# Fused attention and feed-forward kernel: last store by whole rows behind one copy, first scores of both heads of a pair in one step, another order of the first batch's steps

## The chip, the cores and the metric

The kernel runs on one core of one Trainium2 chip. The metric is the device time of one execution in microseconds; the median of three runs before the change is 719.26 us (718.98 to 720.36).

A core has five engines with a queue of instructions each, worked off in order: TensorE (PE, matrix products; its weight loads are listed as PEld), VectorE (DVE), ScalarE (ACT), GpSimd (POOL) and SyncE (SP), which issues all DMA transfers here. Transfers are carried by 16 DMA engines. The engines wait for each other on semaphores. SBUF is the memory on the core with 128 partitions; PSUM holds the results of matrix products, in eight banks.

## The reference

```
p_packed = sm_attn(p, k, v)                 # 32 packed rows per head attend to 576 keys
out      = sm_attn(q, p_packed, p_packed)   # 576 queries attend to the 32 packed rows
x  = out as (8 * 576 tokens, 8 heads * 64)
h  = x @ w_in                               # 512 -> 2048
g  = h * sigmoid(1.702 * h)
return g @ w_out                            # 2048 -> 512
```

`sm_attn` is softmax attention with scale 1/8; there are 8 batches, 8 heads of width 64 and sequence 576. Everything is float32 in DRAM.

## The kernel before

Work goes batch by batch, b = 0 to 7. For each batch the first attention gives the packed rows P (scores1, an exponential, transposes into aT, `pack`, `pack_end`, a transpose into PT), the second gives the attention weights (scores2, maxima, subtraction, exponential, sums, division, transpose). The attention's output isn't formed: PT times w_in is computed instead (`m_chunk`, four chunks fc of 512 columns), and the hidden layer h (128 hidden columns f by 288 tokens, a half) is the product of that with the transposed attention weights (`h_mm`, L561). The gate is a tanh on ScalarE and one VectorE operation. `out_mm` (L621) multiplies the gated values of one f with the rows f of w_out and adds into one of four PSUM banks of 128 tokens each, over f = 0 to 15.

A value that enters the large products is split into an upper part and the rest (`*_upper`, `*_lower`, names ending in hi and lo), and each product is done as three.

576 tokens are four blocks of 128 and 64 more. The 64 left over of two batches make a fifth block (`h_over`, `over_mm`, pairs 0 to 3); its product lands in one bank, `over_take` copies it to SBUF in two halves of 256 columns, and `over_store` stores each half for both batches.

The weights arrive as 64-bit integers' worth of raw bits: `load_w` issues a transfer, `begin_w` (ScalarE) converts the upper bits into a tile `top`, `join_w` (VectorE) puts the value together. Weights are numbered in the order of their queue: 0 to 3 are chunk 0 of w_in, 4 to 7 rows 0 to 3 of w_out, 8 to 11 chunk 1, 12 to 15 rows 4 to 7, 16 to 19 chunk 2, and so on. Weights 0 to 3 come in two halves of columns.

All order is written by hand: `order` is a list of some 2800 steps (a function and its arguments), and a step puts its instructions on the queues of the engines. A step's last argument, such as `dve`, names the engine that does it; otherwise the function's own default holds (ScalarE for copies, POOL for the lower parts). `warm` steps are products without use, on TensorE only; they stand in the first batch. SyncE's queue is in the order of the `load` and `store` steps too, and a transfer into a buffer that is still read waits there with all behind it.

The names used below: `scores1_first` (L247 through `mm1`) computes the first batch's scores of one head of each pair and one half of the keys; `max1_first` L272, `bias1` L302, `exp1_first` L311 turn them into exponentials; `turn1_mm` L337 and `turn1_copy` make aT; `pack` L370; `pack_end` L383 normalises; `scores2_mm` L451, `scores2_turn` L462, `max2` L482, `sub2` L486, `exp2` L490, `sum2` L495, `norm2` L501, `turn2` L507. Copies show as L116 (ScalarE) or L118 (VectorE), conversions of weights as L205, joins as L217.

Of the kernel before, what the change touches and what calls it, by code (L numbers as in the profile page):

```python
# [21 lines left out]
def kernel(  # L22
# [628 lines left out]

    def over_take(pair, k, engine=nc.scalar):
        if k == 0 or pair == B // 2 - 1:
            taken["over"] = o_tile(f"o_over_{pair}_{k}")
        taken["over", pair, k] = o = taken["over"][:, columns(k)]
        move(engine, o, accs[0][:, columns(k)])

    def over_store(pair, k):
        rest = out.rearrange("(b s) d -> b s d", s=S)[2 * pair : 2 * pair + 2, S - REST :, columns(k)]
        nc.sync.dma_start(rest, taken["over", pair, k])  # L660
# [8 lines left out]
        (warm, 2, 3), (warm, 4, 2), (load, "k", 0, 0), (load, "k", 0, 1), (scores1_first, 0, 0),  # L669
        (max1_first, 0, 0), (warm, 6, 2), (scores1_first, 0, 1), (scores1_first, 1, 0),  # L670
        (max1_first, 0, 1), (load_w, 1, 0), (bias1, 0, 0), (exp1_first, 0, 0),
        (scores1_first, 1, 1), (max1_first, 1, 1), (exp1_first, 0, 1), (max1_first, 1, 0),
        (bias1, 0, 1), (sum1, 0, 0), (turn1_mm, 0, 0), (turn1_copy, 0, 0, dve), (load, "v", 0, 0),
        (exp1_first, 1, 0), (exp1_first, 1, 1), (sum1, 0, 1), (load, "v", 0, 1), (warm, 10, 3),
        (turn1_mm, 0, 1), (turn1_last_mm, 0), (turn1_last_copy, 0), (turn1_copy, 0, 1, dve),
        (load_w, 0, 0), (pack, 0, 0, late), (pack, 0, 1), (begin_w, 0, 0), (join_w, 0, 0),
        (pack_end, 0), (pack_turn_mm, 0), (load_w, 2, 0), (begin_w, 2, 0), (join_w, 2, 0),
        (load, "q", 0, 0), (pack_turn_copy, 0), (scores2_mm, 0, 0), (begin_w, 1, 0),
        (load, "q", 0, 1), (join_w, 1, 0), (warm, 7, 3), (scores2_turn, 0, 0, 0),
        (scores2_turn, 0, 0, 1), (max2, 0, 0, 0), (max2, 0, 0, 1), (load_w, 3, 0), (load_w, 3, 1),  # L680
        (begin_w, 3, 0), (sub2, 0, 0, 0, pool), (exp2, 0, 0, 0), (begin_w, 3, 1),
        (scores2_mm, 0, 1, late), (scores2_turn, 0, 1, 0), (join_w, 3, 0),
        (m_chunk, 0, 0, early, 0), (m_upper, 0, 0, 1, 0), (warm, 3, 3), (sub2, 0, 0, 1, pool),
        (scores2_turn, 0, 1, 1), (sum2, 0, 0, 0), (warm, 5, 2), (max2, 0, 1), (join_w, 3, 1),
        (norm2, 0, 0, 0, pool), (turn2, 0, 0, 0), (load_w, 0, 1), (begin_w, 0, 1), (load_w, 4),
        (exp2, 0, 0, 1), (sum2, 0, 0, 1), (warm, 8, 3), (load_w, 6), (begin_w, 4), (join_w, 4),
        (load_w, 1, 1), (sub2, 0, 1, None, pool), (norm2, 0, 0, 1, pool), (a_upper, 0, 0, 0),
        (a_lower_mm, 0, 0, 0, bank_b), (exp2, 0, 1), (sum2, 0, 1), (load_w, 2, 1),
        (turn2, 0, 0, 1), (upper_w, 4), (begin_w, 1, 1), (a_lower_copy, 0, 0, 0),
        (m_upper, 0, 0, 0, 0), (warm, 0, 3), (warm, 9, 3), (m_lower, 0, 0, 0, 0),  # L690
        (a_upper, 0, 0, 1), (a_lower_mm, 0, 0, 1, bank_b), (a_lower_copy, 0, 0, 1),
        (m_lower, 0, 0, 1, 0), (h_mm, 0, 0, 0), (join_w, 0, 1), (norm2, 0, 1, None, pool),
        (turn2, 0, 1), (lower_w, 4), (begin_w, 2, 1), (join_w, 2, 1), (h_tanh, 0, 0, 0),
        (a_upper, 0, 1, None), (a_lower, 0, 1), (h_mm, 0, 1, 0), (h_tanh, 0, 1, 0), (load_w, 5),
        (begin_w, 5), (join_w, 1, 1), (h_gate, 0, 0, 0), (h_gate, 0, 1, 0), (load, "k", 1, 0),
        (h_upper, 0, 0, 0), (h_lower, 0, 0, 0), (m_chunk, 0, 0, (bank_b, bank_b), 1), (load_w, 11),
        (m_upper, 0, 0, 0, 1), (join_w, 5), (upper_w, 5, dve), (m_lower, 0, 0, 0, 1),
        (h_upper, 0, 1, 0), (m_upper, 0, 0, 1, 1), (load_w, 9), (h_mm, 0, 0, 1), (h_tanh, 0, 0, 1),
# [688 lines left out]
```

## Time and profile before

| | |
|---|---|
| runs | 718.98, 719.26, 720.36 us |
| profiled execution: device time / span | 720.15 / 718.4 us |
| granted TensorE clock, mean | 0.995 |
| VectorE, ScalarE, POOL busy | 56%, 39%, 20% of the span |
| read from DRAM, written | 45.60 MB, 9.44 MB |

```profile
DVE  3978885436554366335635457643775547755541
DMA  9787503310203103121110400213210100010001
## 3 DMA queue, kind: packets, MB, share of 16 engines
q1 hardware_dynamic: 17232, 55.05, 22.0%
## 6 DMA issues: line engine op xcount, KB each, us to landing
v<-v SPq DMA_DIRECT2D x8, 1024.0 KB, 5.3
o<-o SPq DMA_DIRECT2D x32, 256.0 KB, 2.3
k<-pk SPq DMA_DIRECT2D x8, 640.0 KB, 3.9
k<-pk SPq DMA_DIRECT2D x8, 576.0 KB, 5.2
```

The first two lines are the busy share in tenths over 40 slices of 18 us each. VectorE and the DMA engines are busiest in the first slices, where weights and the first batch's inputs arrive. The last part lists transfers: what goes where, how many, the size of one, and the median time from issue to landing.

A row of a timeline reads: start, length (us), engine, line, operation, output<-input, shapes, number of instructions merged, and in brackets the idle time before it with what ended it. A float32 product is two instructions, so a `warm` step of 3 shows as x6.

### The profile page before, as it was taken

The numbers are of one execution on the slowest core, as the hardware profiler recorded it, in microseconds if no ns is written. First come the engines' busy times: TensorE is split into PE (matmuls) and PEld (weight loads), VectorE is DVE, ScalarE is ACT, GpSimd is POOL, SyncE is SP. The second block draws the span as 40 slices with busy tenths as digits, with TensorE's granted clock in tenths as the row PEclk, the third lists the DMA queues.
The fourth block names the chain that finished last, engine by engine and source line by source line (L and its number), as shares of the span: only waits on it lengthen the run. The fifth ranks groups of instructions, "written<-read, shape, count | busy, mean of one in ns | idle before, by whom it ended". The sixth has DMA issues, their size and how long they took to land.

```text
span 718.4 us, 13002 instructions
## 1 busy us (share of the span) xinstructions
PE 701.6 (98%) x5092; PEld 569.6 (79%) x5092; DVE 404.4 (56%) x1026; ACT 278.2 (39%) x672; POOL 145.7 (20%) x171
## 2 busy tenths in 40 slices
PE   7999999999999999999999999999999999999994
PEld 5767778878888888888787788877888878888883
DVE  3978885436554366335635457643775547755541
ACT  3777645423323334453322433433342433333220
POOL 1733433122501223222332123102100000000000
PEclk9999999999999999999999999999999999999998
DMA  9787503310203103121110400213210100010001
GB/s 319 311 307 253 189 0 129 96 38 1 81 17 120 39 8 131 43 88 49 60 52 3 165 0 1 96 34 119 69 49 23 66 18 1 16 44 1 1 16 58
DMA packets 17292, 55.87 MB, mean 78 GB/s; under 512 B 1872, under 2 KB 3920, under 8 KB 16208
## 3 DMA queue, kind: packets, MB, share of 16 engines
q1 hardware_dynamic: 17232, 55.05, 22.0%
q8 instruction: 40, 0.66, 0.4%
q14 instruction: 20, 0.16, 0.1%
HBM read 45.60 MB, written 9.44 MB: 77 GB/s over the span
## 4 chain that ended last, share of the span: by engine, by line
PE 93%; DVE 2%; DMA 2%; ACT 1%; issue 0%; SPq 0%; ACTq 0%
PE acc L621 48%; PE h L561 28%; PE acc_over L621 6%; PE psm_None L399 4%; PE pspv L370 2%; DMA raw<-w_in 2%; PE ps L247 1%; PE ps L451 1%; PE pst L337 1%; DMA k<-pk 1%; PE warm L124 1%; ACT top L205 0%; DVE wo L229 0%; DVE w_in L217 0%; DVE mx L482 0%
## 5 line engine op out<-in xcount | busy, mean ns | idle before, releaser
L621 PE MATMUL acc<-wo,ghi 128*128 128x512 f32 x1024 | 323.9, 397 | 1.5 <-DVE ghi L118 0.8
L621 PEld LDWEIGHTS acc<-wo,ghi 128*128 128x128 f32 x1024 | 179.3, 188 | 42.6 <-issue 14.5
L621 PE MATMUL acc<-wo,glo 128*128 128x512 f32 x512 | 201.9, 394 | 0.1
L569 ACT ACTIVATE g<-h 128x288 f32<-128x288 f32 x256 | 104.0, 411 | 242.3 <-PE h L561 226.9
L551 DVE SCALAR_TENSOR_TENSOR g<-g,h 128x288 f32<-128x288 f32 (+1 forms) x256 | 105.4, 416 | 159.0 <-ACT g L569 158.2
L548 POOL TENSOR_TENSOR glo<-g,ghi 128x224 fp32r<-128x224 f32 (+1 forms) x122 | 93.3, 775 | 307.9 <-ACT ghi L116 201.7
L561 PE MATMUL h<-ahi,mhi 128*128 128x288 f32 x512 | 145.5, 299 | 0.9 <-DVE g L551 0.6
L561 PE MATMUL h<-ahi,mlo 128*128 128x288 f32 x512 | 143.0, 295 | 0.0
L621 PEld LDWEIGHTS acc<-wo,glo 128*128 128x128 f32 x512 | 96.1, 188 | 24.0 <-DVE glo L548 0.9
L561 PEld LDWEIGHTS h<-ahi,mhi 128*128 128x128 f32 x512 | 96.2, 188 | 17.9 <-DVE x L462 5.4
L561 PE MATMUL h<-alo,mhi 128*128 128x288 f32 x512 | 108.6, 293 | 0.0
L561 PEld LDWEIGHTS h<-ahi,mlo 128*128 128x128 f32 x512 | 96.3, 188 | 7.0
L116 ACT CAST ghi<-g 128x224 fp32r<-128x224 f32 (+1 forms) x159 | 62.5, 405 | 59.5 <-DVE g L551 37.1
L561 PEld LDWEIGHTS h<-alo,mhi 128*128 128x128 f32 x512 | 82.0, 188 | 0.2 <-POOL alo L530 0.2
L548 DVE TENSOR_TENSOR glo<-g,ghi 128x224 fp32r<-128x224 f32 (+1 forms) x134 | 59.0, 450 | 17.5 <-ACT ghi L116 14.6
L551 DVE SCALAR_TENSOR_TENSOR over<-g,h 128x64 f32<-128x64 f32 x128 | 27.4, 215 | 35.1 <-ACT g L569 34.8
L427 DVE TENSOR_TENSOR mlo<-psm_None,mhi 128x512 fp32r<-128x512 f32 x62 | 42.0, 683 | 5.3 <-ACT mhi L116 4.8
L621 PE MATMUL acc_over<-wo,ghi_over 128*128 128x512 f32 x128 | 39.8, 392 | 0.0
L116 ACT CAST mhi<-psm_None 128x512 fp32r<-128x512 f32 x45 | 26.1, 586 | 30.3 <-PE psm_None L399 30.3
L118 DVE CAST ghi<-g 128x224 fp32r<-128x224 f32 (+1 forms) x97 | 31.6, 333 | 5.6 <-PE acc L621 2.4
L399 PE MATMUL psm_None<-w_in,PT 64*32 64x512 f32 x496 | 34.0, 596 | 0.0
L621 PEld LDWEIGHTS acc_over<-wo,ghi_over 128*128 128x128 f32 x128 | 23.6, 188 | 4.7
(85 smaller groups left out, 498.3 us busy)
## 6 DMA issues: line engine op xcount, KB each, us to landing
q<-q SPq DMA_DIRECT2D x16, 576.0 KB, 5.8
v<-v SPq DMA_DIRECT2D x8, 1024.0 KB, 5.3
o<-o SPq DMA_DIRECT2D x32, 256.0 KB, 2.3
raw<-w_out SPq DMA_DIRECT2D x16, 511.8 KB, 8.2
raw<-w_in SPq DMA_DIRECT2D x12, 511.8 KB, 7.5
k<-pk SPq DMA_DIRECT2D x8, 640.0 KB, 3.9
k<-pk SPq DMA_DIRECT2D x8, 576.0 KB, 5.2
raw<-w_in SPq DMA_DIRECT2D x8, 255.8 KB, 9.8
```

The source lines that it names most:

```text
L116: nc.scalar.copy(dst, src)
L118: engine.tensor_copy(dst, src)
L124: nc.tensor.matmul(t[:, :P], ident, ident, start=True, stop=True)
L247: nc.tensor.matmul(bank[32 * j : 32 * j + 32, :NH], kq["p", b][rows(eo), j, :], kq["k", b][rows(eo), half, j, :], start=True, stop=True,)
L370: nc.tensor.matmul(bank[32 * j : 32 * j + 32, e * D : (e + 1) * D], aT[:kk, c, e, 32 * j : 32 * j + 32], vt[:kk, c, e0 : e0 + D], start=(c ...
L399: nc.tensor.matmul(banks[eo][32 * j : 32 * j + 32, columns(part)], PT[rows(eo), j, :], w_in_sb[fc][rows(eo), j, columns(part)], start=True ...
L427: nc.vector.tensor_tensor(lo, bank[:, at], hi.bitcast(F32), op=ALU.subtract)
L548: engine.tensor_tensor(lo, src, hi.bitcast(F32), op=ALU.subtract)
L551: nc.vector.scalar_tensor_tensor(dst, th, 1.0, h, op0=ALU.add, op1=ALU.mult)
L561: nc.tensor.matmul(h[:, :NH], m[eo][part][:, fo : fo + P], a[:, eo * NH : (eo + 1) * NH], start=(n == 0), stop=(n == len(terms) - 1),)
L569: nc.scalar.activation(g, st["h", b, f, half][:, :NH], AF.Tanh, scale=1.702)
L621: nc.tensor.matmul(acc, gp[:, at : at + P], wo[f][:, part, :], start=(start and i == 0), stop=(stop and i == 2),)
```

## The change

Three things change.

`over_take` makes one copy of the whole bank, 128 partitions by 512 columns, on VectorE. `over_store` stores for one batch 64 whole rows, from 64 partitions. Before it stored 256 columns of both batches' 64 rows.

`scores1_first` takes only the half of the keys and alternates between the two heads of each pair, as `scores1_mm` of the later batches does.

The list of steps up to about step 320 of 2806 is in another order, and 22 of its copies, casts and subtractions go to another engine. It holds the same steps otherwise, with the same number of `warm` products, all of them ahead of the first `h_mm` as before. Behind that the list is the same but for `over_take`.

```
-    def scores1_first(eo, half):
+    def scores1_first(half):
...
-        for j in range(NP):
-            mm1(0, eo, half, bank, j)
-        st["bank", eo, half] = bank
+        for eo in range(2):
+            if half == 0:
+                new1(0, eo)
+            st["bank", eo, half] = (bank_acc(half) if eo else bank_b)(f"ps1_0_{eo}_{half}")
+        for j in range(NP):
+            for eo in range(2):
+                mm1(0, eo, half, st["bank", eo, half], j)
...
-    def over_take(pair, k, engine=nc.scalar):
-        if k == 0 or pair == B // 2 - 1:
-            taken["over"] = o_tile(f"o_over_{pair}_{k}")
-        taken["over", pair, k] = o = taken["over"][:, columns(k)]
-        move(engine, o, accs[0][:, columns(k)])
+    def over_take(pair, engine=nc.scalar):
+        taken["over"] = o_tile(f"o_over_{pair}")
+        move(engine, taken["over"], accs[0])

     def over_store(pair, k):
-        rest = out.rearrange("(b s) d -> b s d", s=S)[2 * pair : 2 * pair + 2, S - REST :, columns(k)]
-        nc.sync.dma_start(rest, taken["over", pair, k])
+        at = (2 * pair + k + 1) * S - REST
+        nc.sync.dma_start(out[at : at + REST, :], taken["over"][k * REST : (k + 1) * REST, :])
...
-        (warm, 2, 3), (warm, 4, 2), (load, "k", 0, 0), (load, "k", 0, 1), (scores1_first, 0, 0),
+        (warm, 8, 3), (warm, 2, 3), (load, "k", 0, 0), (load, "k", 0, 1), (scores1_first, 0),
+        (max1_first, 0, 0), (load, "v", 0, 0), (load, "v", 0, 1), (scores1_first, 1),
...
+        (h_over, 0, 3), (m_upper, 0, 1, 1, None), (load_w, 17),
...
-        (store, 7, 1), (over_take, 3, 0), (over_take, 3, 1, dve), (over_store, 3, 1),
-        (over_store, 3, 0),
+        (store, 7, 1), (over_take, 3, dve), (over_store, 3, 1), (over_store, 3, 0),
```

SyncE's queue at the end of the program, before: the last two ordinary stores, then the two of the fifth block.

```order
L641 DMA o<-o_2_7711 128x512
L641 DMA o<-o_3_7731 128x512
L641 DMA o<-o_0_7703 128x512
L641 DMA o<-o_1_7705 128x512
L660 DMA o<-o_over_1_7778 2x64x256
L660 DMA o<-o_over_0_7776 2x64x256
```

And changed:

```order
L639 DMA o<-o_2_7708 128x512
L639 DMA o<-o_3_7728 128x512
L639 DMA o<-o_0_7700 128x512
L639 DMA o<-o_1_7702 128x512
L655 DMA o<-o_over_7773 64x512 x2
```

The place and the number of stores are the same; their shape is 64x512 instead of 2x64x256, and both read one tile.

VectorE in the first batch, before, from the weight joins (w_in<-raw) ahead of the first scores2 transpose to the transpose of the first normalised quarter (xt). The names: ps are scores2 in PSUM, x their transpose, mx, sm, rs the maxima, sums and reciprocals; 0_0 and 0_1 are the two halves of the queries.

```order
L217 SCALAR_TENSOR_TENSOR w_in_79<-raw_127,top_84 128x256
L462 STREAM_TRANSPOSE x_0_0_237<-ps_0_0_0_238 128x288
L462 STREAM_TRANSPOSE x_0_0_237<-ps_0_0_1_239 128x288
L482 TENSOR_REDUCE mx_0_0_257<-x_0_0_237 128x9 x2
L462 STREAM_TRANSPOSE x_0_1_267<-ps_0_1_0_268 128x288
L217 SCALAR_TENSOR_TENSOR w_in_79<-raw_260,top_86 128x256
L462 STREAM_TRANSPOSE x_0_1_267<-ps_0_1_1_269 128x288
L495 TENSOR_REDUCE sm_0_0_299<-x_0_0_237 128x9
```

And changed, the same stretch, from the two joins ahead of the first transpose:

```order
L217 SCALAR_TENSOR_TENSOR w_in_79<-raw_231,top_83 128x256
L217 SCALAR_TENSOR_TENSOR w_in_79<-raw_160,top_84 128x256
L460 STREAM_TRANSPOSE x_0_0_244<-ps_0_0_0_245 128x288
L480 TENSOR_REDUCE mx_0_0_256<-x_0_0_244 128x9
L460 STREAM_TRANSPOSE x_0_0_244<-ps_0_0_1_246 128x288
L480 TENSOR_REDUCE mx_0_0_256<-x_0_0_244 128x9
L217 SCALAR_TENSOR_TENSOR w_in_79<-raw_240,top_83 128x256
L217 SCALAR_TENSOR_TENSOR w_in_79<-raw_240,top_86 128x256
L493 TENSOR_REDUCE sm_0_0_282<-x_0_0_244 128x9
L494 TENSOR_SCALAR sm_0_0_282<-sm_0_0_282 128x9
L495 RECIPROCAL rs_0_0_283<-sm_0_0_282 128x9
L460 STREAM_TRANSPOSE x_0_1_288<-ps_0_1_0_289 128x288
```

The transposes of the second half (x_0_1) moved behind the two joins of the fourth weight block (raw_240) and the first sums. On TensorE scores2 of the second half (ps_0_1) stands behind the first `m_chunk` now, where it stood ahead of it. A little further on, `m_upper` of one head, a cast of 128x256, has come to VectorE ahead of the first xt.

TensorE from the last hidden product of f = 5 (h_1_5) to the second batch's second scores (ps_1_0_1), before; acc are the banks of the output, ghi and glo the two parts of the gated values of the f named behind, wo the weights.

```order
L561 MATMUL h_1_5_702<-alo_1_386,mhi_1_1_574 128x288
L621 MATMUL acc_0_460<-wo_627,ghi_4_654 128x512 x2
L621 MATMUL acc_0_460<-wo_627,glo_4_655 128x512
L621 MATMUL acc_0_496<-wo_627,ghi_4_654 128x512 x2
L621 MATMUL acc_0_496<-wo_627,glo_4_655 128x512
L247 MATMUL ps_1_0_1_739<-k_404 32x288
```

And changed, from the same hidden product on, without the repeats of the scores:

```order
L559 MATMUL h_1_5_693<-alo_1_388,mhi_1_1_601 128x288
L619 MATMUL acc_0_437<-wo_560,ghi_3_610 128x512 x2
L619 MATMUL acc_0_437<-wo_560,glo_3_611 128x512
L619 MATMUL acc_0_502<-wo_560,ghi_3_610 128x512 x2
L619 MATMUL acc_0_502<-wo_560,glo_3_611 128x512
L247 MATMUL ps_1_0_1_712<-k_535 32x288
```

Ahead of these scores the changed list has no product of f = 4 left; before, the two shown and one ahead of the hidden product stood there. The first now comes right behind the scores.

More of the change, by code (lines that the diff above doesn't have):

```diff
@@ L675 @@
[L675 to L698, printed above, removed]
@@ new lines @@
+        (pack, 0, 1), (pack_end, 0), (pack_turn_mm, 0), (load_w, 0, 0), (pack_turn_copy, 0, dve),
+        (begin_w, 1, 0), (load, "q", 0, 0), (begin_w, 0, 0), (join_w, 0, 0), (load_w, 3, 0),
+        (load_w, 3, 1), (join_w, 1, 0), (scores2_mm, 0, 0), (scores2_turn, 0, 0, 0),
+        (max2, 0, 0, 0), (scores2_turn, 0, 0, 1), (max2, 0, 0, 1), (warm, 4, 2), (begin_w, 3, 1),
+        (join_w, 3, 1), (warm, 6, 2), (begin_w, 3, 0), (join_w, 3, 0), (m_chunk, 0, 0, early, 0),
+        (sub2, 0, 0, 0, pool), (exp2, 0, 0, 0), (sum2, 0, 0, 0), (load, "q", 0, 1),
@@ new lines @@
+        (load_w, 11), (begin_w, 11), (join_w, 11), (load_w, 10), (begin_w, 10), (join_w, 10),
+        (load, "k", 1, 0), (scores1_mm, 1, 0, inner), (h_upper, 0, 2, 0), (scores1_max, 1, 0, 0),
+        (lower_w, 6), (h_upper, 0, 2, 1), (h_lower, 0, 2, 1), (scores1_copy, 1, 0, 0),
+        (scores1_max, 1, 0, 1), (upper_w, 7), (lower_w, 7), (scores1_copy, 1, 0, 1),
+        (m_chunk, 0, 1), (m_upper, 0, 1, 0, None, dve), (m_lower, 0, 1, 0), (h_mm, 0, 3, 0),
+        (h_tanh, 0, 3, 0), (h_gate, 0, 3, 0), (h_mm, 0, 3, 1), (out_mm, 0, 2, 3),
@@ new lines @@
+        (h_gate, 2, 4, 1), (h_mm, 2, 5, 0), (h_tanh, 2, 5, 0), (h_gate, 2, 5, 0),
+        (h_lower, 2, 4, 0), (h_mm, 2, 5, 1), (h_tanh, 2, 5, 1), (h_gate, 2, 5, 1), (h_over, 2, 5),
+        (h_upper, 2, 5, 0, dve), (over_store, 0, 1), (h_upper, 2, 5, 1, dve),
+        (h_lower, 2, 5, 1, dve), (out_mm, 2, 4, 0), (h_upper, 2, 4, 1), (h_lower, 2, 5, 0, dve),
+        (m_chunk, 2, 2), (load, "k", 3, 1), (scores1_mm, 3, 1, inner), (scores1_max, 3, 1, 1),
+        (m_upper, 2, 2, 0, None), (m_lower, 2, 2, 0), (bias1, 3, 1), (scores1_copy, 3, 1, 0),
@@ new lines @@
+        (m_chunk, 6, 1), (m_upper, 6, 1, 0, None, dve), (scores1_max, 7, 0, 1),
+        (m_upper, 6, 1, 1, None, dve), (m_lower, 6, 1, 1), (store, 5, 0), (m_lower, 6, 1, 0),
+        (out_mm, 6, 1, 1), (out_mm, 6, 2, 1), (h_mm, 6, 3, 1), (out_mm, 6, 1, 2),
+        (scores1_copy, 7, 0, 1), (out_mm, 6, 2, 2), (h_tanh, 6, 3, 1), (h_gate, 6, 3, 1),
+        (h_over, 6, 3), (out_mm, 6, 1, 3), (out_mm, 6, 2, 3), (h_mm, 6, 4, 0), (h_mm, 6, 3, 0),
+        (h_tanh, 6, 4, 0), (h_gate, 6, 4, 0), (h_tanh, 6, 3, 0), (h_gate, 6, 3, 0),
```

250 lines of the change are left out of this document (121 added, 129 removed).

## The prediction

> **What bounds the kernel now.** I read the page first, then busy time by stretch, then the end of the chain of waits, then the engines' timelines of the first 60 us.
>
> ```profile
> span 718.4 us, 13002 instructions
> PE 701.6 (98%) x5092; PEld 569.6 (79%) x5092; DVE 404.4 (56%) x1026; ACT 278.2 (39%) x672; POOL 145.7 (20%) x171
> ```
>
> ```profile
> 0.00:30.00 30.00, 25.29 (x263) 1.00 0.95 354
> 30.00:60.00 30.00, 28.51 (x192) 1.00 0.79 273
> 300.00:500.00 200.00, 199.79 (x1508) 1.00 0.18 60
> ```
>
> TensorE is the bound, and in the middle it is full: 199.79 us busy of 200. Nothing done there for other engines can move the end. What can be won lies in three places: before TensorE starts the long run of products (4.7 us not busy in the first 30), in its pauses between 30 and 60 us (1.5 us), and the time behind its last product (from 708.8 to 718.4, next rows). The profiled run took 720.15 us, 0.9 above the median of 719.26; I work out differences on the profiled run and apply their sum to the median.
>
> **The tail: one copy, two stores of whole rows.** First the end of the chain of waits, then the timeline of the copy and of SyncE's issues:
>
> ```profile
> 697.74 11.02 PE acc_over L621 x48
> 708.82 0.38 ACT o_over L116
> 709.23 0.42 DVE o_over L118
> ```
>
> ```profile
> 700.51 0.68 DVE L118 COPY o<-acc 128x512 f32<-128x512 f32 x1
> 701.22 1.31 SPq L641 DMA_DIRECT2D o<-o  x3
> 709.68 1.14 SPq L660 DMA_DIRECT2D o<-o_over  x2
> ```
>
> The last product ends at 708.8. The two half-width copies run one behind the other (the VectorE copy starts when the ScalarE copy ends) and are done at 709.65, 0.83 us after the first began. One full-width VectorE copy has a row: 0.68. So the issue can begin at 709.5, 0.15 earlier. What follows is larger. The transfers in quarter-microsecond stretches (us, clock, share of the 16 DMA engines, GB/s):
>
> ```profile
> 710.65:710.90 0.25, 1.00 0.06 16
> 716.65:716.90 0.25, 0.50 0.14 49
> 717.15:717.40 0.25, 0.50 0.00 0
> ...
> 702.00:702.25 0.25, 1.00 0.81 303
> 703.75:704.00 0.25, 1.00 1.04 393
> ```
>
> The last stores start moving about 1.0 us after SyncE began the first issue and then crawl for 6.3 us at a share of 0.13 to 0.14, which is two engines' worth of sixteen, and 49 GB/s. Three ordinary stores (128 rows of 2 KB, issued at 701.22) move at 393 GB/s. The last two have the shape 2x64x256, the ordinary ones 128x512. The new ones are 64x512. No store of that shape is in the trace, but a load is, with nothing queued behind it:
>
> ```profile
> 366.47 0.52 SPq L152 DMA_DIRECT2D v<-v_last  x1
> ...
> 368.50:368.75 0.25, 1.00 0.14 49
> 368.75:369.00 0.25, 1.00 0.00 0
> ```
>
> That load is 128 KB, 64 partitions by 512. At 49 GB/s it would need 2.7 us; it is over 2.3 us after its issue began, of which about 0.9 passes before data move. So a 64x512 transfer isn't held to two engines. I take 393 GB/s for the new stores: 0.33 us each. First issue at 709.5, second at 710.0 (0.52 each, by the row of the load), its data from 711.0 to 711.35. From the last byte (716.95) to the end of the span pass 1.45 us, which stay. End at 712.8 instead of 718.4: **-5.6 us**. Ends of the range: 393 GB/s and shorter issues give -6.0; the old rate with only the copy's gain gives -0.15.
>
> [...]
>
> The same two edits for pairs 0 to 2 cost nothing: one 0.68 copy takes the place of a 0.42 and a 0.37, in stretches where TensorE is full. If that cover were gone each would be worth about 0.1 us.
>
> **The head, up to the first hidden-layer product (L561, at 26.60 now).** TensorE's work is the same set of products in both, so after that point only pauses can differ.
>
> ```profile
> 4.77 1.18 PE L247 MATMUL ps<-k 64*32 64x288 f32 x8 [0.91 <-DMA k<-pk]
> 7.04 2.17 PE L247 MATMUL ps<-k 64*32 64x288 f32 x24
> 13.40 2.53 PE L370 MATMUL pspv<-v,aT 128*32 128x64 f32 x80
> 37.97 0.71 PE L247 MATMUL ps<-k 64*32 64x288 f32 x16
> ```
>
> ```profile
> 9.10 0.50 ACT L311 ACTIVATE x<-ps,nb 128x288 f32<-128x288 f32 x1 [6.67 <-DVE nb L302]
> 16.00 0.31 ACT L383 ACTIVATE pn<-pspv,rs 128x64 f32<-128x64 f32 x1 [0.76 <-PE pspv L370]
> 16.90 1.11 ACT L205 CAST top<-raw 128x256 f16<-128x256 bf16 x2
> ```
>
> ```profile
> 4.50:5.00 0.50, 1.00 1.11 433
> ```
>
> Scores: 32 instructions take 1.18 + 2.17 = 3.35 us with one head at a time; 16 with both heads alternating take 0.71 in the second batch. But the early clock is slower, by the means of the same 128x128 product in two windows:
>
> ```profile
> L124 PE MATMUL warm<-ident 128*128 128x128 f32 x6 | 1.5, 421 | 0.0
> L124 PE MATMUL warm<-ident 128*128 128x128 f32 x12 | 1.5, 275 | 0.0
> ```
>
> So 0.71 becomes about 1.1 there (x 421/275). The first half of the keys lands at 4.77 as now. The second half (576 KB behind it, at 433 GB/s) lands near 6.1, while TensorE uses it only at 7.04 now. So the second half's scores start 0.9 us earlier, take 0.35 longer than one head's, and the first exponential moves from 9.10 to about 8.5. From there to the second half of the packed product the steps are the same, on other queues: three warm products still lie between the two sets of transposes, and the aT copies go to ScalarE, which is free there. I take -0.5 us for the end of that product: normalising its second half (16.00) begins at 15.5. Ends: -1.5 (keys at 5.9, the clock faster sooner) to +0.3 (keys just before 7.04).
>
> Of the loads only the order changes: v goes ahead of the weight halves. The queue is full either way (share 0.95, 354 GB/s in the first 30 us, above): the 3.8 MB up to q's first half take 10.8 us, the next 1.1 MB (two weight halves, q's second half) 3.1 more, so both are there before their products at about 16.6 and 20.6. That costs nothing; were the queue 4 us later, the second would.
>
> Then VectorE decides, which had no pause from 17.42 on:
>
> ```profile
> 17.42 0.42 DVE L217 SCALAR_TENSOR_TENSOR w_in<-raw,top 128x256 uint32<-128x256 uint32 x1 [0.28 <-ACT top L205]
> 17.86 0.85 DVE L462 STREAM_TRANSPOSE x<-ps 128x288 f32<-128x288 f32 x2
> 19.37 0.48 DVE L462 STREAM_TRANSPOSE x<-ps 128x288 f32<-128x288 f32 x1
> 25.40 0.42 DVE L507 STREAM_TRANSPOSE xt<-x 128x288 f32<-128x288 f32 x1
> 44.07 0.33 DVE L118 CAST ghi<-g 128x288 fp32r<-128x288 f32 x1
> ...
> 18.57 0.71 PE L451 MATMUL ps<-q,PT 64*32 64x288 f32 x16
> 20.22 0.62 PE L399 MATMUL psm<-w_in,PT 64*32 64x256 f32 x4 [0.52 <-DVE w_in L217]
> 26.60 0.30 PE L561 MATMUL h<-ahi,mhi 128*128 128x288 f32 x1
> ```
>
> Two weight conversions, 1.11 on ScalarE, now come behind the second normalising activation, and their joins, 0.42 each on VectorE, ahead of the first score transpose: 15.5 + 0.3 + 1.1 + 0.84 = 17.75, against 17.86 now. The 0.5 won before is spent. From that transpose to the last one before the hidden layer VectorE now needs 25.40 - 17.86 = 7.54 us. It gets one cast more (m_upper of a half chunk, 128x256, priced at the 0.33 of a 128x288 cast). It also gets a wait. The second scores2 product now stands behind the first m_chunk, whose last pair needs the join of the fourth weight block, at about 20.1 by VectorE's queue; its 0.6, then 0.8 from the scores' start to their transpose (18.57 to 19.37) give 21.4, when VectorE has been free for 0.5 us. Queued behind that transpose are the maximum, the cast, the transpose of the normalised quarter and both sums; POOL's next subtraction waits with them. Sum: -0.1 + 0.33 + 0.5 = +0.7 us, first hidden product at 27.3. Ends: -0.8 (no wait, lead kept) to +1.5.
>
> **The pauses after it.**
>
> ```profile
> 50.74 0.50 PE L621 MATMUL acc<-wo,ghi 128*128 128x512 f32 x1 [0.71 <-POOL wo L229]
> 53.74 0.73 PE L621 MATMUL acc<-wo,ghi 128*128 128x512 f32 x2 [0.78 <-DVE ghi L118]
> 51.37 2.03 ACT L205 CAST top<-raw 128x512 f16<-128x512 bf16 x3 [2.41 <-DMA raw<-w_in]
> ```
>
> The pauses, 0.71 and 0.78, are the whole 1.5 us that TensorE misses between 30 and 60. Both belong to products of f = 4, whose weights or hidden values stood on POOL and VectorE behind joins and casts, and these behind ScalarE conversions that waited for weight loads (2.41 us in the third row). In the changed order the f = 4 products come only after the second batch's second scores, and two weight loads of the third chunk (17 and 18) are issued ahead of those that wait for a buffer (12 to 15). I take both pauses as gone: **-1.5 us**. Ends: -2.2 (0.6 more from the scores there, whose 16 instructions are stretched) to +1.0, if the new order waits for something else.
>
> **Sum.** -5.6 + 0.7 - 1.5 = -6.4 us. On the median: 719.26 - 6.4 = **712.9 us**.
>
> **Rivals.**
> 1. *The head gives nothing or loses.* VectorE's queue ahead of the hidden layer loses the 1.5 us and the pauses come back elsewhere: +1.5 and -0.5, so -4.6 and 714.7; with a new 1 us pause 716. For it speaks that VectorE has no idle row there; against it that it sheds two aT copies (0.68 each, by the copy of that shape above).
> 2. *The head gains more.* The lead of the scores is kept (-0.8) and the pauses go (-2.2): 710.7. Needs scores that are done well before 7.0.
> 3. *The stores stay on two engines.* Then only the copy is won, -0.15, with the head's -0.8: 718.3. Their 2 KB rows could halve the 6.3 us: 715. The 64x512 load speaks against it.
> 4. *Slower.* TensorE's early products are slow (421 against 275 ns) and its stream there is thinner now: alternating scores finish sooner, so it idles longer. If it stays slow into the dense part from 27 us, every us of old work costs 0.5 more. It eats the -6.4 and shows as slower only when some 15 us of that part's work run slow, which gives about 721. The granted clock reads 1.00 in both windows, so only such means show it. Against it: the 275 ns are from 23.8 to 25.5 us, when TensorE still runs mostly filler; the 421 ns are from 2.1 to 2.9. A small chance. [...]
>
> **How the numbers follow.** Forecast 66%, at 712.9 with its own range 711.2 to 714.3. Rival 1 14%, rival 2 13%, rival 3 5% (half of it at 718.3, half near 715), rival 4 2%. The range 710.6 to 715.6 takes in rival 2 and most of rival 1 and leaves out 2 in 10, as sizes in the head are worked out over many short steps. A measurement tells about 0.2% (1.4 us) from no change; below 717.8 is faster: 94%. Within 0.2%: 4%, from rival 3 and a mix of 3 and 1. Slower: 2%.
>
> **What would show it.** Right: a share near 1.0 of the DMA engines for under 1 us after the last copy, the span ending about 3 us after that copy; first L561 near 27.3; no L229 or ghi pause of TensorE between 45 and 55 us. Wrong: a share of 0.13 again after the last product; L561 before 26 or after 28.5; new pauses over 0.5 us between 30 and 75 us; 128x128 products at 421 ns past 20 us.

## The result and the profile after

| | before | after |
|---|---|---|
| median of four runs each, us | 719.51 (718.98 to 720.36) | 715.05 (714.48 to 715.8) |
| profiled execution: device time / span | 720.15 / 718.4 | 715.8 / 714.0 |

The ratio is 0.9938, with an interval of 0.992 to 0.9955: 4.5 us faster, where 6.4 were forecast.

The page of the changed kernel, its first lines, and TensorE's busy time by stretch (from:to in us, length, busy us, number of instructions, clock, share of the DMA engines, GB/s):

```profile
span 714.0 us, 12980 instructions
...
PE 700.0 (98%) x5092; PEld 568.5 (80%) x5092; DVE 404.5 (57%) x1027; ACT 276.1 (39%) x668; POOL 144.7 (20%) x170
```

```profile
0.00:30.00 30.00, 23.79 (x271) 1.00 0.96 366
30.00:60.00 30.00, 29.86 (x209) 1.00 0.75 266
60.00:100.00 40.00, 38.05 (x324) 1.00 0.41 146
300.00:500.00 200.00, 199.25 (x1499) 1.00 0.18 60
```

TensorE is still the bound. Between 30 and 60 us it now misses 0.14 us instead of 1.5. But between 300 and 500 it misses 0.75 instead of 0.21: something was lost in the part that was taken as full.

**The tail.** VectorE's copy and SyncE's issue in the timeline, then the last stretches with DMA traffic (busy times of the five engines, clock, DMA share, GB/s):

```profile
708.86 0.40 PE L619 MATMUL acc_over<-wo,glo_over 128*128 128x512 f32 x1
709.34 0.69 DVE L118 COPY o_over<-acc_over 128x512 f32<-128x512 f32 x1 [6.57 <-PE acc_over L619]
710.06 1.11 SPq L655 DMA_DIRECT2D o<-o_over  x2
```

```profile
711.25:711.50 0.25, 0.00 (x0) 0.00 (x0) 0.00 (x0) 0.00 (x0) 0.00 (x0) 1.00 0.90 205
...
712.00:712.25 0.25, 0.00 (x0) 0.00 (x0) 0.00 (x0) 0.00 (x0) 0.00 (x0) 1.00 1.06 221
712.25:712.50 0.25, 0.00 (x0) 0.00 (x0) 0.00 (x0) 0.00 (x0) 0.00 (x0) 1.00 0.71 156
```

All 16 engines work (share 0.9 to 1.06 instead of 0.13), as forecast, but at 205 to 221 GB/s, about half of the 393 that the forecast took. The last product ends at 709.25 and the span at 714.02: 4.8 us, where 9.6 stood before and 4.0 were forecast.

**The head.** TensorE's first products (the row at 25.25 is the first hidden product), then VectorE's transposes from the first scores2 to the last one ahead of the hidden layer:

```profile
4.86 1.21 PE L247 MATMUL ps<-k 64*32 64x288 f32 x16 [0.57 <-DMA k<-pk]
6.25 1.21 PE L247 MATMUL ps<-k 64*32 64x288 f32 x16 [0.18 <-DMA k<-pk]
...
11.46 1.73 PE L368 MATMUL pspv<-v,aT 128*32 128x64 f32 x80
25.25 0.29 PE L559 MATMUL h<-ahi,mhi 128*128 128x288 f32 x1
```

```profile
8.37 0.50 ACT L309 ACTIVATE x<-ps,nb 128x288 f32<-128x288 f32 x1 [5.94 <-DVE nb L300]
13.45 0.52 ACT L381 ACTIVATE pn<-pspv,rs 128x64 f32<-128x64 f32 x2 [1.51 <-DVE rs L326]
...
15.54 0.48 DVE L460 STREAM_TRANSPOSE x<-ps 128x288 f32<-128x288 f32 x1
24.05 0.42 DVE L505 STREAM_TRANSPOSE xt<-x 128x288 f32<-128x288 f32 x1
```

The first exponential is at 8.37 (forecast 8.5). The two normalising activations stand in one row, from 13.45 to 13.97; the second, for which 15.5 was forecast, starts near 13.66 (16.00 before). The 80 products of `pack` take 1.73 us instead of 2.53, because products of the same shape turn faster from about 10 us on instead of 15: TensorE's clock rose earlier, as "The early clock" below reads it. VectorE's stretch from 15.54 to 24.05 is 8.51 us long (forecast 7.54 + 0.33 + 0.5 = 8.37). So the first hidden product comes 1.35 us earlier than before, not 0.7 later.

**The pauses.** Those at 50.74 and 53.74 are gone. Two others stand in the second batch's first attention, where the kernel before had none (in e1_again, the same kernel once more, only the second is left, with 0.46 us):

```profile
67.67 0.66 PE L335 MATMUL pst<-ident,x 128*128 128x128 f32 x4 [0.47 <-ACT x L316]
72.09 1.15 PE L368 MATMUL pspv<-v,aT 64*32 64x64 f32 x48 [0.79 <-ACT aT L116]
```

**Where the lead goes.** Each batch has one packed transpose (`pspt`). Its start is a mark in the stream of TensorE, and the start of the last pair's `acc_over` products is the last mark. One such row of the changed kernel:

```profile
74.07 0.27 PE L387 MATMUL pspt<-ident,pn 128*128 128x128 f32 x1
```

| start, us | batch 2 | batch 3 | batch 5 | batch 7 | batch 8 | last acc_over |
|---|---|---|---|---|---|---|
| before | 76.29 | 157.76 | 324.42 | 492.65 | 588.49 | 697.57 |
| after | 74.07 | 155.78 | 322.87 | 492.56 | 588.76 | 698.03 |
| after less before | -2.22 | -1.98 | -1.55 | -0.09 | +0.27 | +0.46 |

A lead of 2.2 us at 74 us is a lag of 0.5 at 697. Part of it goes in one step at 376 us, part in an even creep. In sum the span is 4.4 us shorter: 4.9 from the tail, less 0.5. The early lead differs between executions of one kernel, the loss behind it hardly: e1_again leads by 3.13 at the second batch (73.16) and by 0.52 at the end (697.05), a loss of 2.6 where this execution loses 2.7.

The step has these rows, VectorE's and TensorE's, in the changed kernel:

```profile
376.23 0.67 PE L247 MATMUL ps<-k 64*32 64x288 f32 x2
376.34 0.69 DVE L118 COPY o_over<-acc_over 128x512 f32<-128x512 f32 x1 [2.59 <-PE acc_over L619]
376.94 0.44 DVE L549 SCALAR_TENSOR_TENSOR g<-g,h 128x288 f32<-128x288 f32 x1
...
377.44 0.47 PE L247 MATMUL ps<-k 64*32 64x288 f32 x7 [0.55 <-DVE g L549]
```

Pair 1's copy of the fifth block waits on VectorE for the last `acc_over` product, and a gate (g) is queued behind it. The second head's scores need the PSUM bank that this gate reads. Before, the copy's first half ran on ScalarE and its second half stood behind the gate, so the gate was free of it.

### The profile page after: what moved, and what is told of

The parts are those of the page before. It is cut to its first block, busy times and chain, and to the rows that moved or that the text cites. A ratio compares the mean times of both kernels' runs of the same rounds, so it can differ in the third digit from the quotient of the medians.

```text
span 714.0 us, 12980 instructions
## 1 busy us (share of the span) xinstructions
PE 700.0 (98%) x5092; PEld 568.5 (80%) x5092; DVE 404.5 (57%) x1027; ACT 276.1 (39%) x668; POOL 144.7 (20%) x170
## 4 chain that ended last, share of the span: by engine, by line
PE 91%; DVE 4%; DMA 2%; ACT 1%; issue 0%; SPq 0%; DVEq 0%; ACTq 0%
PE acc L619 48%; PE h L559 28%; PE acc_over L619 6%; PE psm_None L397 4%; PE pspv L368 2%; DMA raw<-w_out 1%; PE ps L247 1%; PE ps L449 1%; PE pst L335 1%; DVE w_in L217 1%; DMA k<-pk 1%; ACT top L205 1%; DVE x L460 0%; DVE wo L229 0%; PE warm L124 0%
## 5 line engine op out<-in xcount | busy, mean ns | idle before, releaser
L546 POOL TENSOR_TENSOR glo<-g,ghi 128x288 fp32r<-128x288 f32 (+1 forms) x119 | 89.7, 764 | 313.4 <-ACT ghi L116 205.5
L116 ACT CAST ghi<-g 128x288 fp32r<-128x288 f32 (+1 forms) x161 | 63.3, 406 | 60.5 <-DVE g L549 37.9
L546 DVE TENSOR_TENSOR glo<-g,ghi 128x288 fp32r<-128x288 f32 (+1 forms) x137 | 60.4, 451 | 18.8 <-ACT ghi L116 16.0
```

The lines of the kernel that those rows point to most:

```text
L116: nc.scalar.copy(dst, src)
L546: engine.tensor_tensor(lo, src, hi.bitcast(F32), op=ALU.subtract)
```

## The experiments

They ran on three chips: e1 to e4 on one, e5 to e8 on a second, e9 to e12 on a third. The kernel before, timed beside them, had medians of 719.25, 719.13 and 719.0 us there. Each ratio is to the kernel before on the same chip. A difference in us between two experiments of different chips holds what the chips differ by as well, so the places and the clock are judged by marks on one chip where there are any.

**The changed kernel again**, as the base for the others.

> The changed kernel once more, beside the kernel before on the same chip. If the 1.4 us that the changed profile loses evenly between 100 and 700 us against the profile of before lies in the two profiled executions and not in the change, the new profile's steady stretch (from the second batch's pspt, 74.07, to the last acc_over product, 709.27, in the first profile) is shorter than 635.2 us by up to 1.4. If the change itself slows the steady part, it stays at 635.2. The first 128x128 products at 275 ns come near 10.5 us again if the early clock is settled by the order of work, and anywhere from 7 to 15 us if it depends on the moment the program starts.

715.06 us (714.79 to 715.13), ratio 0.9935 [0.9923, 0.9948].

**The tail alone.** The kernel before, with only the last pair's copy and stores in the new form:

```
-        (store, 7, 1), (over_take, 3, 0), (over_take, 3, 1, dve), (over_store, 3, 1),
-        (over_store, 3, 0),
+        (store, 7, 1), (over_take_whole, 3, dve), (over_store_whole, 3, 1),
+        (over_store_whole, 3, 0),
```

> The kernel before with only the last pair's copy and stores changed (pairs 0 to 2 keep their two half copies and 2x64x256 stores). Theory (the tail is worth 4.9 by the two profiles: 9.66 us from the last product to the end before, 4.73 after): 4.9 us faster than before, ratio 0.993. Rival (stores of 64 rows don't gain, or the head made the difference): under 1 us. My blind term was 5.6.

714.5 us (714.23 to 714.63), ratio 0.9928 [0.9914, 0.9941]: 4.75 us less than before. The tail alone gives all of the gain; the rest of the change together gives nothing, or costs half a microsecond.

**The first batch alone.** The changed kernel with the old `over_take` and `over_store` (and pair 1's two copies on both sides of the gate again):

```
-        (over_mm, 1, 3), (over_take, 1, dve), (h_gate, 4, 2, 0),
+        (over_mm, 1, 3), (over_take, 1, 0), (h_gate, 4, 2, 0), (over_take, 1, 1, dve),
```

> The changed kernel's first scores and order of steps with the old over_take and over_store everywhere. Theory: TensorE leads by 2.2 us at the second batch's pspt and keeps it, as the wait of 1.2 us behind pair 1's whole copy is gone: 2.2 us faster than before, ratio 0.997, no TensorE wait on a gate between 300 and 400 us. Rival (the lead is lost in the steady part whatever the copies do): 0 to 0.7 us faster. Blind terms for the head: +0.7 - 1.5 = 0.8 faster.

718.65 us (718.0 to 719.39), ratio 0.9991 [0.9982, 0.9999]: 0.6 us less than before. Its profile has a lead of 3.07 us at the second batch (73.22) and of 1.52 at the last `acc_over` (696.05). There is no step at 376 us here, so half of the lead is lost by the creep alone.

**Pair 1's copy behind the gate.**

```
-        (h_tanh, 4, 2, 0), (over_mm, 1, 3), (over_take, 1, dve), (h_gate, 4, 2, 0),
+        (h_tanh, 4, 2, 0), (over_mm, 1, 3), (h_gate, 4, 2, 0), (over_take, 1, dve),
```

> The changed kernel with two neighbouring steps exchanged: h_gate 4 2 0 ahead of pair 1's over_take on VectorE. Theory (the copy waits for the last over product and holds up the gate, which holds a PSUM bank that the second batch's fifth scores need): TensorE's wait at 377 us goes and the kernel is 1.0 to 1.2 us faster than the changed kernel, about 713.9. Rival (something else, the bank or a load, sets that wait): same as the changed kernel, within 0.3 us.

714.19 us (713.3 to 714.31), ratio 0.992 [0.9908, 0.9932]: 0.87 us less than e1_again on the same chip. The stretch from the second batch's mark to the last `acc_over` takes 622.73 us instead of 623.89. The step is gone; VectorE has the gate first, and all 16 score instructions follow in one go:

```profile
374.15 0.45 DVE L549 SCALAR_TENSOR_TENSOR g<-g,h 128x288 f32<-128x288 f32 x1 [0.81 <-ACT g L567]
...
375.82 0.72 PE L247 MATMUL ps<-k 64*32 64x288 f32 x16
375.93 0.69 DVE L118 COPY o_over<-acc_over 128x512 f32<-128x512 f32 x1 [1.33 <-PE acc_over L619]
```

The parts add up: -4.75 (tail) - 0.6 (first batch) + 0.9 (pair 1's copy) = -4.45, and e1_again is 4.2 below the kernel before.

**The creep: where the tiles lie.** The pools hand out SBUF addresses in the order in which tile names are first used. The new order of the first batch therefore moves most work tiles to other addresses: ghi from 157344 to 161440, mhi of head 0 from 141600 to 112928, and 13 of the 16 places of w_out. The first test takes each tag once, ahead of everything, in the old order of first use (43 tags; the instructions stay those of e4_gate_first):

```
+    places = (
+        ("kqv", 2560, 2), ("x", 576, 5), ("mx1", 2, 2), ("wo13", 1024, 1), ("nb1", 1, 2),
...
+    )
+    for tag, n, bufs in places:
+        for i in range(bufs):
+            wk.tile([P, n], F32, tag=tag, name=f"place_{tag}_{i}", bufs=bufs)
```

> The instructions and their order are those of e4_gate_first; only the SBUF addresses of the work tiles are put back to those of the kernel before (each tag is given its place in the old order of first use). Theory 'places': in the runs with the changed first batch the same steady products take 0.2% longer between 75 and 700 us, 1.2 to 1.4 us in all, because their operands lie elsewhere; then this run is 1.0 to 1.4 us faster than e4_gate_first (ratio to before about 0.991, 712.8 to 713.2 us where before is 719.2), and its lead over before does not shrink from 75 us on outside the places where the order differs. Rival 'order or state': the drift follows from how the first batch runs or leaves the clock; then this run gives e4_gate_first's time again (0.993, within 0.4 us) and the drift is there as it was.

712.06 us (711.72 to 713.29), ratio 0.9906 [0.9893, 0.992]: 2.1 us less than e4_gate_first, which ran on another chip. That is more than expected, and the marks say why (e8 is described below; its first batch and its places are those of e4, its chip is that of e5):

| start, us | batch 2 | batch 3 | batch 5 | batch 7 | batch 8 | last acc_over |
|---|---|---|---|---|---|---|
| e4, new places | 73.69 | 155.42 | 322.48 | 491.00 | 587.17 | 696.42 |
| e8, new places | 72.58 | 154.23 | 321.29 | 489.81 | 585.99 | 695.20 |
| e5, old places | 72.58 | 154.12 | 320.90 | 489.08 | 584.98 | 694.05 |

e8 and e5 are level at the second batch and 1.15 us apart at the end, evenly gained: the creep hangs on the places. The 1.1 us between e4 and e8 at the second batch is another thing, the early clock (below). The waits don't make the creep. TensorE was busy 589.60 us of the 590 between 100 and 690 in e8 and 589.61 in e5, at a granted clock of 1.00 in both. It is the products themselves that take longer, as the groups of the two kernels show (instructions, busy us, mean ns), e8 first:

```profile
L619 PE MATMUL acc<-wo,glo 128*128 128x512 f32 x451 | 178.3, 395 | 0.1
L559 PE MATMUL h<-alo,mhi 128*128 128x288 f32 x452 | 96.0, 294 | 0.0
```

```profile
L634 PE MATMUL acc<-wo,glo 128*128 128x512 f32 x453 | 178.7, 394 | 0.0
L574 PE MATMUL h<-alo,mhi 128*128 128x288 f32 x452 | 95.7, 293 | 0.0
```

A nanosecond of 394, and 0.3 us in one group (the `acc` group of e8 has less busy time only because it has two instructions fewer in the window): too little to catch the eye, but over 4200 products it makes the 1.15 us.

**The same the other way round**: e2_tail_only, with tags taken in the new order of first use.

> e2_tail_only (first batch as before) with the work tiles at the SBUF addresses that the changed kernel has; instructions and order are e2_tail_only's. Theory 'places', the other way round: the steady products take 0.2% longer, the lead against e2_tail_only falls evenly by 1.2 to 1.4 us between 75 and 700 us, and the time is 1.0 to 1.5 us above it (715.5 to 716.0 where e2_tail_only had 714.5). Rival: the drift needs the changed order too; then 714.5 within 0.4.

714.6 us (714.32 to 715.16), ratio 0.9938 [0.9925, 0.9951]: within the noise the time of e2_tail_only (ratio 0.9928, on another chip). By its time the rival holds; the marks show a creep all the same:

| start, us | batch 2 | batch 3 | batch 5 | batch 7 | batch 8 | last acc_over |
|---|---|---|---|---|---|---|
| e2, old places | 75.42 | 156.87 | 323.60 | 491.81 | 587.67 | 696.75 |
| e10, new places | 73.95 | 155.62 | 322.67 | 491.06 | 587.27 | 696.52 |
| e10 less e2 | -1.47 | -1.25 | -0.93 | -0.75 | -0.40 | -0.23 |

The creep of 1.2 us came with the places, without the changed order. But e10 is 1.5 us ahead at the second batch. Its first hidden product comes 0.3 us earlier (25.61 against 25.91), and two pauses behind it came out smaller by 0.73; 0.4 us stay unexplained. The first two rows are e2's, the third is e10's; its second pause is gone:

```profile
50.23 0.50 PE L621 MATMUL acc<-wo,ghi 128*128 128x512 f32 x1 [0.91 <-POOL wo L229]
52.86 0.73 PE L621 MATMUL acc<-wo,ghi 128*128 128x512 f32 x2 [0.41 <-DVE ghi L118]
```

```profile
49.62 0.50 PE L636 MATMUL acc<-wo,ghi 128*128 128x512 f32 x1 [0.59 <-POOL wo L244]
```

Whether the smaller pauses also follow from the places, or from the clock, which rose about half a microsecond sooner in this execution, one profile can't tell. What the places give or take ahead of the long stretch stays open.

In the long stretch they decide. From the second batch's mark to the last `acc_over` the executions without the step at 376 us need (those not met yet follow below):

| us | old places | new places |
|---|---|---|
| chip of e1 to e4 | 621.33 (e2) | 622.83 (e3), 622.73 (e4) |
| chip of e5 to e8 | 621.47 (e5), 621.39 (e6) | 622.54 (e7), 622.62 (e8) |
| chip of e9 to e12 | 621.57 (e9), 621.57 (e12) | 622.57 (e10) |

On each chip the new places cost 1.0 to 1.5 us. The old order stands in both columns (e2 and e6, e10), and so does the new one; the kernel before, with the old places, has 621.28.

**Which tiles.** e5_same_places with only the 16 places of w_out exchanged among themselves:

```
-        ("kqv", 2560, 2), ("x", 576, 5), ("mx1", 2, 2), ("wo13", 1024, 1), ("nb1", 1, 2),
+        ("kqv", 2560, 2), ("x", 576, 5), ("mx1", 2, 2), ("wo14", 1024, 1), ("nb1", 1, 2),
...
```

> e5_same_places with only the 16 places of the output weights (wo) exchanged among themselves (10 of 16 moved, in the order of first use of the changed kernel); all other tiles stay at the places of before. Theory 'weights': the drift comes from where the moving weights of the output products lie; then 0.7 to 1.4 us of it is back by 700 us (712.7 to 713.5). Rival 'the split operands' (mhi, mlo, ahi, alo, ghi, glo, which lie as before here): no drift against e5_same_places (712.1 within 0.4).

712.68 us (711.9 to 713.1), ratio 0.9909 [0.9894, 0.9924]. It is 0.50 us behind e5_same_places at the second batch (73.08 against 72.58) and 0.60 at the last `acc_over`; its long stretch, 621.57, is that of e9 and e12 on its own chip. So this exchange makes no creep. The split operands' places (m, a and g) and those of the small tiles are the likely ones left; they weren't tested, nor were the weights at the very addresses of the changed kernel. Why places matter isn't known.

**One store on two engines.** e4_gate_first with the two 64x512 stores written as one:

```
-        (over_store, 3, 1), (over_store, 3, 0),
+        (over_store_once, 3),
...
+        rest = out.rearrange("(b s) d -> b s d", s=S)[2 * pair : 2 * pair + 2, S - REST :, :]
+        nc.sync.dma_start(rest, taken["over"])
```

> e4_gate_first with the two last stores of 64x512 written as one store of 2x64x512: the same rows of 2 KB, the same bytes, but the slowest dimension is 2. Theory 'count of engines': it lands on two DMA engines like the stores of before (49 GB/s), 262 KB take about 5.3 us instead of 1.5, and the kernel is 3.5 to 4.5 us slower than e4_gate_first (717.7 to 718.7), nearly the time of before. Rival 'row size': what was slow before were rows of 1 KB and four transfers; then the store takes 1.2 to 1.5 us as in e4_gate_first and the time stays within 0.4 us of 714.2.

718.51 us (717.71 to 720.43), ratio 0.9992 [0.9981, 1.0002]: 4.3 us above e4_gate_first. That one ran on another chip, but the profiles agree: from the last product to the end of the span pass 9.6 us, against 4.8 in e4 and in e5. The same rows of 2 KB, now with a slowest dimension of 2, crawl again. One of its last stretches (busy times of five engines, clock, DMA share, GB/s):

```profile
714.00:714.50 0.50, 0.00 (x0) 0.00 (x0) 0.00 (x0) 0.00 (x0) 0.00 (x0) 0.50 0.13 49
```

So it isn't the row's length that made the old stores slow. With a slowest dimension of 2 the share is 0.13, two engines' worth of sixteen, and 49 GB/s move; with 64, in the changed kernel, the share is 0.9 to 1.06, at 205 to 221 GB/s.

**Both halves at once.** e5_same_places with the second store issued by ScalarE's queue:

```
-        (over_store, 3, 1), (over_store, 3, 0),
+        (over_store, 3, 1), (over_store, 3, 0, act),
```

> e5_same_places with the second of the last two stores issued from ScalarE's queue instead of SP's, so that both 64x512 stores are issued together. [...]

711.9 us (711.19 to 712.77), ratio 0.9899 [0.9883, 0.9914]. Both issues begin at 705.79. The stretches behind them (busy time of TensorE, clock, DMA share, GB/s):

```profile
707.25:707.50 0.25, 0.00 (x0) 1.00 1.09 205
707.50:707.75 0.25, 0.00 (x0) 1.00 0.81 279
707.75:708.00 0.25, 0.00 (x0) 1.00 0.76 287
```

At 0.78 of the engines' time 283 GB/s move, where one store alone had 205 to 221 at a share near 1.0. The last product (704.98) to the end of the span (709.4) takes 4.43 us instead of the 4.77 of e5_same_places: 0.3 won. One 64-partition store had about half of the 393 GB/s that the 128-partition stores had in the kernel before, and the two at once, from partitions 64 to 127 and 0 to 63, stay below 393. No run here explains either.

**The early clock.** Two tests open or fill an idle stretch of TensorE ahead of the first score transpose. Opened, on e4_gate_first:

```
-        (max1_first, 0, 1), (bias1, 0, 0), (warm, 7, 3), (exp1_first, 0, 0), (exp1_first, 0, 1),
+        (max1_first, 0, 1), (bias1, 0, 0), (warm, 7, 1), (exp1_first, 0, 0), (exp1_first, 0, 1),
```

> e4_gate_first with one filler product instead of three ahead of the first score transpose, so that TensorE stands idle for about 1 us at 8 to 9 us. Theory 'unbroken work': the clock then rises near 14.2 us (5.2 us after 9.0) instead of 10.0, the 80 products of stage A take 2.3 to 2.5 us instead of 1.73, the packed product comes 0.9 to 1.5 us later than 14.0, and the time is 0.2 to 0.9 us above e4_gate_first (714.2). Rival 'density' (the paired scores alone bring the clock up) or 'set from outside': the rise stays near 10 us and nothing else moves; the time stays within 0.2 us.

715.41 us (714.98 to 716.02), ratio 0.9951 [0.9937, 0.9964], 1.2 us above e4_gate_first, which ran on another chip. TensorE's rows:

```profile
9.09 1.17 PE L335 MATMUL pst<-ident,x 128*128 128x128 f32 x4 [0.81 <-ACT x L309]
12.75 2.28 PE L368 MATMUL pspv<-v,aT 128*32 128x64 f32 x80
15.46 0.33 PE L387 MATMUL pspt<-ident,pn 128*128 128x128 f32 x1 [0.43 <-ACT pn L381]
```

The transposes start 0.3 us later than in e4_gate_first (8.80), the packed transpose 1.5 later (13.99): the clock rose at 14.0 instead of 10.4. Against e8_store_once, which has the same first batch but for the two fillers, the same places and the same chip, the second batch's mark comes 2.2 us later (74.78 against 72.58) and the last `acc_over` 2.1 (697.32 against 695.20). So two filler products fewer cost 1.2 to 2.2 us, as far as two executions tell.

Filled, on e2_tail_only:

```
-        (bias1, 0, 1), (sum1, 0, 0), (turn1_mm, 0, 0), (turn1_copy, 0, 0, dve), (load, "v", 0, 0),
-        (exp1_first, 1, 0), (exp1_first, 1, 1), (sum1, 0, 1), (load, "v", 0, 1), (warm, 10, 3),
+        (bias1, 0, 1), (sum1, 0, 0), (warm, 12, 1), (turn1_mm, 0, 0), (turn1_copy, 0, 0, dve), (load, "v", 0, 0),
+        (exp1_first, 1, 0), (exp1_first, 1, 1), (sum1, 0, 1), (load, "v", 0, 1), (warm, 10, 2), (warm, 13, 1),
```

> The kernel e2_tail_only (first batch as before) with one filler product more, put ahead of the first score transpose, where TensorE stood idle for 0.53 us at 9.21 us; the three fillers after the transpose are written as 2 and 1. Theory 'unbroken work': the clock rose at 15.1 us before and at 10.0 us after because that is 5.1 to 5.4 us behind the last idle stretch of 0.5 us or more (ends at 9.74 and at 4.86); with the stretch filled, the 128x128 products go from 421 to 275 ns near 10 us, the 80 products of stage A take 1.73 us instead of 2.53, and the packed product is 0.8 to 1.5 us earlier than 16.37; the time is 0.2 to 0.8 us below e2_tail_only (714.5). Rival 'set from outside': the clock rises at 15 us as before whatever TensorE does, the filler delays the transposes by 0.1 to 0.4 us, and the time is e2_tail_only's or up to 0.3 above.

713.86 us (712.91 to 715.24), ratio 0.9931 [0.9918, 0.9945]. The median is 0.64 us below e2_tail_only's on another chip, but the ratio to the kernel before is no better than its 0.9928. The 80 products took 1.78 us and the clock rose at 13.4. But in e2_tail_only, whose first batch is that of the kernel before, they took 1.85 and it rose at 13.6, not at 15.3 as in the profile of before. Filling this gap did nothing that can be told from chance, so "5.2 us after the last idle stretch" is not the rule.

What all profiles show together, read off where the same products turn faster (128x128 from 421 to 275 ns, the 80 from 314 to 222): with the old first batch the clock rose at 15.3, 13.6, 13.4 and about 13 us; with the new one (with the heads apart too) at 10.0 to 10.4 in four executions and somewhere between 4.3 and 6.2 in five; with the opened gap at 14.0. The granted clock of the profile reads 1.00 in all these stretches, so that it is a clock is inferred from the products' lengths alone. The first scores of e4_gate_first and of e8_store_once, the same first batch, differ by it:

```profile
6.05 1.21 PE L247 MATMUL ps<-k 64*32 64x288 f32 x16 [0.19 <-DMA k<-pk]
```

```profile
6.19 0.72 PE L247 MATMUL ps<-k 64*32 64x288 f32 x16 [0.31 <-DMA k<-pk]
```

The program shifts the moment: on each of the three chips the old order rose later than the new one (13.6 against 10.0 to 10.4; 13.4 against 4.3 to 6.2; about 13 against 4.3 to 5.5). The program alone doesn't fix it. But all executions of the new order at 10.0 to 10.4 are the first result and e1 to e4, and all the earlier ones are e5 to e12: whether the spread is one between executions or one between chips isn't shown. What makes the clock rise isn't shown either, and the 4 us or more between e4 and e8 stay unexplained.

**The heads apart again**, on e5_same_places:

```
-        for j in range(NP):
-            for eo in range(2):
+        for eo in range(2):
+            for j in range(NP):
                 mm1(0, eo, half, st["bank", eo, half], j)
```

> e5_same_places with the first scores of the two heads of a pair one head after the other again inside each half (same instructions, only their order on TensorE). Theory 'pairing': two heads side by side take 1.21 us for 16, one head alone takes 1.18 for 8, so each half's scores end 1.1 to 1.2 us later; the first half's overrun pushes the second half, and the first exp, at 8.3 to 8.4 us, comes 0.9 to 1.3 us later; the packed product follows by as much or more, since the clock's rise may come later too; the time is 0.5 to 1.3 us above e5_same_places (712.1). Rival: the head waits for the loads of the keys and values, not for the scores; then the packed product moves by under 0.3 us and the time stays within 0.3 us.

711.98 us (711.68 to 712.15), ratio 0.9899 [0.9884, 0.9913]: no difference from e5_same_places, nor from e9_two_queues on its own chip. The clock was up after the first half here (1.06 us for its 16 instructions), and the second half took the 0.72 that it takes with the heads paired:

```profile
4.71 1.06 PE L262 MATMUL ps<-k 64*32 64x288 f32 x16 [0.43 <-DMA k<-pk]
6.17 0.72 PE L262 MATMUL ps<-k 64*32 64x288 f32 x16 [0.39 <-DMA k<-pk]
```

So the alternation inside the step isn't needed: the 16 instructions take the same time one head behind the other, and TensorE waited 0.39 us for the second half of the keys in any case. The step still has both heads of one half behind each other, which the order before hadn't, and the clock was fast; neither was taken apart.

**The best version** is that of e9_two_queues: the changed kernel with pair 1's gate ahead of the copy, the old places, and the last two stores from two queues. It is 7.1 us faster than the kernel before on its chip (ratio 0.9899). The median is 3.1 below that of the changed kernel, but part of this is the earlier clock of e5 to e12, which may hang on the chip. e5_same_places and e12_heads_apart stand within 0.2 us of it, which the times can't tell apart.

## Why the prediction was right, and where its sizes were off

The time, 715.05, lies in the range, and the sign and the main term, the tail, are right. It lies above the forecast's own 711.2 to 714.3, where rival 1 stood. The forecast of 712.9 was 2.1 us too low. On the profiled execution it is 2.0, in these parts: tail 0.7 less than forecast, first 75 us 1.4 more, the long stretch 2.7 lost that the sum had at nothing. That the total came so near is in part luck: the 1.4 us, which came from a cause outside the sum, hid half of the 2.7.

- *Tail, -5.6.* It is -4.9 in the profile and -4.75 alone (e2_tail_only). The reading of the shape held: a share of 0.13 before and of 0.9 to 1.06 after, and in e8_store_once the same rows of 2 KB with a slowest dimension of 2 had 0.13 again. The mis-sized term is "393 GB/s for the new stores: 0.33 us each". That rate was taken from a store of 128 partitions; from 64 it is 205 to 221 GB/s and about 0.65 us each, so the span ends 4.0 us after the copy and not about 3. The 64x512 load that was called as witness only bounded the rate from below. The stretch 368.00 to 368.25 of the trace of before, just ahead of the two that the prediction shows of that load, moved 205 GB/s (the last bytes of stores issued ahead of it may be among them).
- *"The same two edits for pairs 0 to 2 cost nothing."* This step failed. The copy's length was weighed, not what is queued behind it: pair 1's copy now stands ahead of a gate, and scores that need the gate's bank stopped TensorE. It cost 0.9 us (e4_gate_first).
- *Head, first stage, -0.5.* It came out at -2.3 (the second half's normalising near 13.66 instead of 16.00). The scores' part was right: keys at 6.25, first exponential at 8.37. The clock was what was missing; it rose 5 us sooner. With the rise put off to 14.0 (e7_open_gap) the packed transpose comes at 15.46 instead of before's 16.37, close to the forecast. The prediction looked at the clock only as a danger (rival 4), and it went the other way. The trace of before shows the slow clock ending at 15.3 us, where the 80 products go from 314 to 219 ns. That the two heads alternate carried nothing in e12_heads_apart, under the fast clock.
- *Head, VectorE's stretch, 7.54 + 0.33 + 0.5.* Right in size: 8.51 against 8.37. The first hidden product at 25.25 is still outside the 26 to 28.5 that the prediction gave as its signs, as the stage ahead of it ended earlier.
- *Pauses, -1.5.* Both are gone, as said, and 0.47 and 0.79 come back at 67 and 72 us; the second is over the 0.5 us that was named as a sign of being wrong. From the first hidden product to the second batch's mark this execution takes 48.82 us instead of 49.69, 0.9 less. But e1_again takes 47.85, 1.8 less, and e10_tail_new_places, with the old order, 48.34: one pair of profiles doesn't size this term. With the first stage the lead at the second batch is 2.2 us, where 0.7 - 1.5 gives 0.8.
- *"Nothing done there for other engines can move the end."* This step failed too, twice: the gate above is work of VectorE that did move the end, and the places moved it without any wait. From 100 to 690 us TensorE was busy all but 0.4 us in e5 and in e8, and 1.15 us came from products that each took a fraction of a nanosecond longer, after the tiles had changed places (e10 against e2 shows the same).
- *Rivals.* The time is near the 714.7 of "the head gives nothing", and in e3_head_only the head gave only 0.6. But VectorE's queue, which that rival blamed, behaved as forecast; the lead was won by the clock and the pauses and lost later.

## What to carry to other kernels

Look at the slowest dimension of a store that stands at the end of a program, where nothing covers it: 64 instead of 2 was worth 4.3 to 4.9 us here. The rate still differed: 205 to 221 GB/s from 64 partitions, 393 from 128. When a copy goes to another engine, look at what is queued behind it there, even where its engine has time to spare. And when tiles are first used in another order, compare their addresses as well, or fix them: on this kernel, bound by TensorE, the places alone moved the long stretch by 1.0 to 1.5 us, half of the lead that the first batch's new order had won in e3_head_only.

## What was not expected of the hardware

- The same products on other SBUF addresses ran 0.2% longer (1.15 us of 621, e8 against e5), with TensorE fully busy in both, and likewise on the two other chips. The addresses of the large tiles kept their remainder by 64 bytes (32, as the 157344 and 161440 of ghi); exchanging ten of the places of w_out among themselves didn't do it. The cause is open.
- The clock's rise lay between 4.3 and 10.4 us with one first batch, and between about 13 and 15.3 with the other. Between e4 and e8, on two chips, it was worth 1.1 us at the second batch's mark; between e7 and e8, on one chip, 2.2.
- A store of 64 partitions kept all 16 DMA engines busy at 205 to 221 GB/s, and two of them at once, from both halves of the partitions, reached 279 to 287.
